# Attention ahead of a mixture of experts on one core: a planner's prices, the port of VectorE and GpSimd in its books, and a margin for attention's matmuls

## The chip, the cores and the metric

The kernel runs on one core of a Trainium2 chip. The metric is the device time of one execution in microseconds; the time before is 980.52 us, the median of 3 runs (980.38 to 980.91).

The engines are named as in the profile: PE is TensorE's matmul queue and PEld its weight loads, DVE is VectorE, ACT is ScalarE, POOL is GpSimd, SP is SyncE, which issues the loads. Each engine takes its instructions in the order of the program and waits for the others by semaphores.

## The reference

Windowed attention with ALiBi biases, and on its output a mixture of four experts whose weights come from given probabilities. All in float32:

```python
B, H, S, D = 4, 8, 576, 64            # q, k, v: (B, H, S, D)
scores = np.matmul(q, k.T) / 8 + slope[h] * -abs(i - j)
scores = np.where((i >= j) & (i - j < 128), scores, -1e9)
attn = softmax(scores)                # rows divided by (sum + 1e-9)
x = np.matmul(attn, v)                # to (2304 tokens, 512)
p = domain_probs / (domain_probs.sum(-1, keepdims=True) + 1e-9)
for e in range(4):                    # w1: (4, 512, 1024), w2: (4, 1024, 512)
    h = np.maximum(x @ w1[e], 0.0)
    out += p[:, e:e + 1] * (h @ w2[e])
```

## The kernel before, in words

**Precision.** A product of two float32 matrices is made of three products in a faster format: every operand is split into a high part (a cast, L278 on ScalarE or L280 on VectorE) and a low part (the difference to the operand, L288, on VectorE or GpSimd), and high by high, high by low and low by high are summed in PSUM. So each weight, each query, key, value, probability and activation costs a cast and a difference on its way to TensorE.

**Tokens and experts.** The 2304 tokens are cut into seven blocks, three of 256 and four of 384. A pass over the weights serves some of the blocks; weights are loaded in 16 units of 256 hidden features (tiles `w1r`, `w2r`, two places each), split (`w1h`, `w1l`, `w2h`, `w2l`) and used. For a unit and a block, `hidden` makes two tiles of hidden features: 12 matmuls in two halves of 6 (L761; the first half needs the heads' pairs 0 and 1, the second half pairs 2 and 3), then ScalarE's relu (L782) and VectorE's low part (L789). `output` multiplies them by w2, 6 matmuls per tile of 128 tokens (L823), and VectorE adds the result, weighted, to an accumulator in SBUF (L840). The first 12 units begin before all of attention is there: units 0 to 6 on block 0 alone, 7 to 11 on blocks 0 and 1, 12 to 15 on blocks 0 to 2. Blocks 3 and 4 share one pass, 5 and 6 the last.

**Attention.** It is done by block and pair of heads, in tiles of 128 queries (72 in all); block 0 works on float32 as it is, the others on split operands. The chain of a tile in `unit` is:

- scores on TensorE (L446; in block 0 L437) into a PSUM bank;
- the scores of the previous tile's keys copied to `s` (L278 or L280), those of its own keys by a predicated copy (L482);
- for each of the two heads, bias and minimum on VectorE (L492), the exponentials and their sums on ScalarE (L504);
- sums plus 1e-9 and their reciprocal on VectorE (L520, L529), then the scaling, in one instruction on VectorE (L536) or in two on ScalarE (L544);
- two transposes on TensorE (L569), high and low part (L278 or L280, L288), and two masked copies on GpSimd into `pt` (L599, L586);
- products with the values on TensorE (L635), summed over the tiles of the segment in PSUM, brought together by ScalarE and VectorE (L658, L661), and split into `xh` and `xl`, which the experts read.

There are three places for `s`, two for the parts, three for `pt`, six PSUM banks for everything but the value products.

**What sets the order.** Nothing is written out by hand. Every operation is first noted with the engines that can do it, an estimate of its time on each, and a due time (`Plan.op`). `Plan.order` then simulates the engines: for each, it looks for the operations that could start first (within `SLACK`, 0.1 us), takes the most urgent by due time, gives an operation that several engines can do to the one that ends it sooner, and records a start. A start is the latest of: the engine being free, the operands being ready (end of each producer plus `GAP`, a passing time by pair of engines, plus `EXTRA`), and a place in the pools being free. Sorted by these starts, the instructions are emitted. The due times of the experts are a running sum of their matmuls' estimated time; those of attention are spread between the times at which blocks are opened, 10 us early (`MARGIN`). The simulation only sets the order: on the chip each engine waits for what its next instruction needs.

The estimates of before are the lines that the change touches:

```python
pool = lambda n: 0.1 + n * 0.0022  # noqa: E731
mm = lambda n: max(n / 2400 + 0.0025, 0.107)  # noqa: E731
```

Of the kernel before, what the change touches and what calls it, by code (L numbers as in the profile page):

```python
# [26 lines left out]
# The operations are noted first, with what they read and write, an estimate of their time and when they are due; a  # L27
# greedy simulation of the engines then sets the order in which they are emitted.
class Buf:
    """A tile of the program: it takes one of its tag's places from its first use to its last."""  # L30
# [8 lines left out]
class Op:  # L39
    __slots__ = ("n", "engs", "emit", "due", "deps", "outs", "wait", "ready", "bufs", "cold", "start", "end", "eng")  # L40


class Plan:
    # What passes from the end of one engine's operation to the start of another's that waits for it.
# [11 lines left out]
    def op(self, engs, emit, due, reads=(), writes=(), holds=(), cold=None):  # L56
        """engs: the engines that can do it, with the time there (us; of a load its bytes)."""
        o = Op()
        o.n, o.engs, o.emit, o.due = len(self.ops), dict(engs), emit, due
        o.deps, o.outs, o.bufs, o.start = set(), [], [], None  # L60
        o.cold = 2 * o.engs.get(PE, 0.0) if cold is None else cold
# [23 lines left out]
    def order(self):  # L85
        at = dict.fromkeys((PE, DVE, ACT, POOL, SP), 0.0)
        queue = {e: [] for e in at}
        bus = 0.0
        owner = {tag: [None] * len(p) for tag, p in self.places.items()}

        def push(o):
            o.ready = {e: max((d.end + EXTRA + self.GAP[d.eng][e] for d in o.deps), default=0.0) for e in o.engs}
            for e in o.engs:
                queue[e].append(o)

        def slots(o):
            """When there are places for what starts with it, and which."""
# [22 lines left out]
        while len(out) < len(self.ops):  # L120
            best = None
            for e, q in queue.items():
                cands, least = [], None
                for o in q:
                    s = slots(o)
                    if s is None:
                        continue
                    t = max(at[e], o.ready[e], s[0] + 0.2 if s[1] else 0.0)
                    cands.append((t, o, s[1]))
                    least = t if least is None else min(least, t)  # L130
# [5 lines left out]
                # Where another engine would end it sooner, it is left to that one.  # L136
# [20 lines left out]
            else:  # L157
                o.end = t + (o.cold if e == PE and t < 10.0 else o.engs[e])
                at[e] = o.end
            new = [b for b in o.bufs if b.place is None]  # L160
# [16 lines left out]
EXTRA = 0.03  # L177

# Time of an instruction on n elements a partition (us).
act = lambda n: 0.05 + n * 0.00087  # noqa: E731  # L180
dve = lambda n: 0.065 + n / 960  # noqa: E731
dve2 = lambda n: 0.065 + n / 1920  # noqa: E731
pool = lambda n: 0.1 + n * 0.0022  # noqa: E731
mm = lambda n: max(n / 2400 + 0.0025, 0.107)  # noqa: E731
mmc = lambda n: max(n / 1200, 0.107)  # noqa: E731

# Blocks of tokens (a pass of the weights takes some of them), and the columns of their group's tile.
# [11 lines left out]
def attention_moe(  # L199
# [14 lines left out]
    P = 128  # L214
# [58 lines left out]
    def cast(o, i, n, due, reads, writes, sbuf=True):  # L273
        """A copy: on ScalarE or VectorE."""
# [7 lines left out]
        plan.op({ACT: act(n), DVE: dve2(n) if sbuf else dve(n)}, emit, due, reads, writes)  # L282

    def minus(o, a, b, n, due, reads, writes, gp=True):
        """A difference: on VectorE, or on GpSimd where both are in SBUF."""
# [4 lines left out]
        plan.op({DVE: dve(n), POOL: pool(n)} if gp else {DVE: dve(n)}, emit, due, reads, writes)  # L290

# [1 line left out]
    # Units of two tiles of hidden features on some blocks of tokens: the first block starts before the others.  # L293
# [21 lines left out]
    def before(t):  # L315
        """How many keys of the tile before a tile's own its scores need; sequences may start in a tile's middle."""
        return min(t * P % S, P)

    # Blocks between whose starts the attention of the next ones is spread.
# [29 lines left out]
    def segment(g):  # L349
        """Loads of the operands, and their high and low parts: queries and keys stacked along the contraction."""  # L350
# [6 lines left out]
        if g.plain:  # L357
            # Both at once: these are what all the others wait for.
# [52 lines left out]
        v4 = lambda: v[:].rearrange("p t (h d) -> p t h d", h=2)[:, :vn]  # noqa: E731  # L411
# [12 lines left out]
    def unit(u):  # L424
# [5 lines left out]
        sv = lambda: s[:, : 2 * P].rearrange("p (h n) -> p h n", h=2) if s.tag == "acc" else s.place  # noqa: E731  # L430
        both = [(s, 0), (s, 1)]
        sc = lambda: bk[:].rearrange("p (h n) -> p h n", h=2)  # noqa: E731
# [21 lines left out]
        # One column for each key of the window: that of the query's tile up to the query, else that of the tile before.  # L454
        # Where a sequence ends in a tile, the queries past it see none of its keys.
# [6 lines left out]
        if pk and (pk < P or edge):  # L462
            plan.op({DVE: 0.28, POOL: 0.3}, clear, d, ["scores"], both)
        qk = [g.q, g.k] if g.plain else [g.qs, g.kh, g.kl]
        passes_ = 8 if g.plain else 4
        plan.op({PE: passes_ * mm(n)}, scores, d, qk, [bk, "scores"], [s], passes_ * mmc(n))
# [23 lines left out]
        # Negated scores and their minimum, the exponentials and their sums.  # L490
# [22 lines left out]
        for h in range(2):  # L513
            keys = [("bias", g.hp)] if pk else [("bias0", g.hp), bk]
            plan.op({DVE: 0.205}, least(h), d + 0.3, keys, [(s, h), (t, h)])
        for h in range(2):
            plan.op({ACT: 0.38}, exponents(h), d + 0.4, [(t, h)], [(s, h), (t, 2 + h)])
        plan.op(
            {DVE: 0.07},
# [499 lines left out]
```

## Time and profile before

| | |
|---|---|
| median of 3 runs | 980.52 us |
| span of the profiled execution | 977.4 us |
| TensorE, matmuls busy | 925.4 us, 95% of the span |
| VectorE busy | 754.0 us, 77% |
| ScalarE busy | 352.2 us, 36% |
| GpSimd busy | 285.6 us, 29% |
| mean granted TensorE clock | 0.995 |

The span runs from the first to the last instruction of the execution that was profiled; the time of a run also holds what lies around it, 3.1 us beside the median. Matmuls overlap in the pipeline, and their ends are modelled, so a row's length is longer than the distance to the next start. A wait is written behind the instruction that waited, with the engine, tile and line that ended it. In a group's row stand the count, the busy time, the mean in ns and the idle time ahead of it.

### The profile page before, as it was taken

To read this page: it belongs to the slowest core of one execution; us is meant where nothing else is said; L and a number is where in the kernel's file an instruction comes from. 1 tells how busy PE (TensorE), PEld (TensorE's weight loads), DVE (VectorE), ACT (ScalarE), POOL (GpSimd) and SP (SyncE) were. 2 spreads that over 40 slices of the span, in tenths; PEclk is the share of its full clock that TensorE was granted. 3 is DMA by queue.
4 is the path that set the end of the run, shared out by engine and by line. 5 is a ranking of instruction groups with operands and counts; after the bars stand their busy time and mean duration, and the time that the engine had idled before them with its cause. 6 is when DMAs were issued, how large, how long until landed. Compare 5 with 4: busy or idle time off the path is not lost.

```text
span 977.4 us, 14432 instructions
## 1 busy us (share of the span) xinstructions
PE 925.4 (95%) x5222; PEld 829.9 (85%) x5222; DVE 754.0 (77%) x1575; ACT 352.2 (36%) x909; POOL 285.6 (29%) x278
## 2 busy tenths in 40 slices
PE   6788898999999999999999999999999999999998
PEld 4677787888888888988888889899999999999997
DVE  5999998898889899888797787866656565656554
ACT  4655445344454555333233432343221212121210
POOL 4667543334434255322232232222101010101000
PEclk9899999999999999999999999999999999999999
DMA  9655433232333345422222211111321121211101
GB/s 235 195 173 171 143 135 114 92 105 84 106 128 117 123 144 191 138 92 83 74 92 82 74 65 58 52 44 65 103 91 66 51 76 46 67 63 65 44 1 65
DMA packets 38359, 95.67 MB, mean 98 GB/s; under 512 B 3728, under 2 KB 15888, under 8 KB 38288
## 3 DMA queue, kind: packets, MB, share of 16 engines
q1 hardware_dynamic: 38288, 94.75, 29.3%
q8 instruction: 41, 0.67, 0.3%
q14 instruction: 30, 0.25, 0.1%
HBM read 90.02 MB, written 4.72 MB: 97 GB/s over the span
## 4 chain that ended last, share of the span: by engine, by line
PE 67%; DVE 26%; issue 3%; DMA 2%; ACT 1%; POOL 1%; DVEq 0%; ACTq 0%; POOLq 0%; SPq 0%
PE b L761 31%; PE b L823 30%; DVE s L492 5%; DVE acc L840 3%; DVE w2l L288 3%; PE av L635 2%; DVE w1l L288 2%; PE b L569 2%; DVE rl L789 2%; DVE qs L288 2%; PE b L446 2%; DVE s L536 1%; DVE s L482 1%; DMA k<-in_qk 1%; DVE x L661 1%
## 5 line engine op out<-in xcount | busy, mean ns | idle before, releaser
L761 PE MATMUL b<-xh,w1h 128*128 128x384 f32 (+1 forms) x896 | 286.8, 320 | 0.0
L761 PE MATMUL b<-xl,w1h 128*128 128x384 f32 (+1 forms) x896 | 281.7, 314 | 0.2 <-DVE xl L288 0.2
L761 PE MATMUL b<-xh,w1l 128*128 128x384 f32 (+1 forms) x896 | 281.7, 314 | 0.0
L840 DVE SCALAR_TENSOR_TENSOR acc<-b,prob,acc 128x512 f32<-128x512 f32 (+1 forms) x271 | 201.7, 745 | 64.9 <-PE b L823 64.2
L782 ACT ACTIVATE rh<-b 128x384 fp32r<-128x384 f32 (+1 forms) x224 | 98.9, 442 | 402.8 <-PE b L761 400.4
L823 PE MATMUL b<-w2l,rh 128*128 128x512 f32 x578 | 227.4, 394 | 0.0
L823 PE MATMUL b<-w2h,rl 128*128 128x512 f32 x578 | 226.9, 393 | 0.0
L823 PE MATMUL b<-w2h,rh 128*128 128x512 f32 x578 | 226.4, 392 | 0.0
L789 DVE SCALAR_TENSOR_TENSOR rl<-b,rh 128x384 fp32r<-128x384 f32 (+1 forms) x224 | 111.0, 495 | 103.8 <-ACT rh L782 102.7
L761 PEld LDWEIGHTS b<-xl,w1h 128*128 128x128 f32 x896 | 170.6, 190 | 5.8 <-DVE xl L288 0.4
L761 PEld LDWEIGHTS b<-xh,w1h 128*128 128x128 f32 x896 | 170.8, 191 | 5.3
L288 POOL TENSOR_TENSOR w1l<-w1r,w1h 128x512 fp32r<-128x512 f32 x60 | 83.6, 1394 | 305.2 <-DVE w1h L280 212.1
L761 PEld LDWEIGHTS b<-xh,w1l 128*128 128x128 f32 x896 | 170.3, 190 | 0.0
L823 PEld LDWEIGHTS b<-w2h,rl 128*128 128x128 f32 x578 | 108.5, 188 | 23.6
L823 PEld LDWEIGHTS b<-w2h,rh 128*128 128x128 f32 x578 | 109.1, 189 | 15.8
L823 PEld LDWEIGHTS b<-w2l,rh 128*128 128x128 f32 x578 | 108.9, 188 | 15.5
L599 POOL TENSOR_SCALAR_AFFINE_SELECT pt<-hl 128x512 fp32r<-128x512 f32 x60 | 42.6, 710 | 235.3 <-DVE hl L288 208.5
L504 ACT ACTIVATE s<-s,t 128x128 f32<-128x128 f32 x128 | 50.8, 398 | 81.8 <-DVE t L492 80.7
L492 DVE CUSTOM_DVE_ANT_0 s<-s,bias 128x128 f32<-128x128 f32 x120 | 75.7, 654 | 1.1
L288 DVE TENSOR_TENSOR w2l<-w2r,w2h 128x512 fp32r<-128x512 f32 x102 | 76.0, 770 | 0.0
L278 ACT ACTIVATE w2h<-w2r 128x512 fp32r<-128x512 f32 x117 | 71.6, 625 | 8.2 <-PE b L823 6.5
L280 DVE CAST w1h<-w1r 128x512 fp32r<-128x512 f32 x92 | 58.8, 653 | 17.5 <-PE b L761 16.2
(89 smaller groups left out, 924.9 us busy)
## 6 DMA issues: line engine op xcount, KB each, us to landing
w1r<-in_w SPq DMA_DIRECT2D x60, 512.0 KB, 3.5
w2r<-in_w SPq DMA_DIRECT2D x60, 512.0 KB, 3.5
q<-in_q SPq DMA_DIRECT2D x16, 384.0 KB, 3.3
k<-in_k SPq DMA_DIRECT2D x12, 512.0 KB, 4.1
k<-in_k SPq DMA_DIRECT2D x12, 384.0 KB, 3.4
out<-acc SPq DMA_DIRECT2D x17, 256.0 KB, 2.0
v<-in_v SPq DMA_DIRECT2D x12, 256.0 KB, 2.7
v<-in_v SPq DMA_DIRECT2D x12, 192.0 KB, 3.0
```

Source lines behind the costliest of these rows:

```text
L278: nc.scalar.activation(o(), i(), AF.Copy)
L280: nc.vector.tensor_copy(o(), i())
L288: by[e].tensor_tensor(out=o(), in0=a(), in1=f(b()), op=ALU.subtract)
L446: nc.tensor.matmul(sc()[:, h, :n], g.qs[:, h, u.q0 : u.q0 + P], m[:, h, u.k0 : u.k0 + n], start=m is g.kh, stop=m is g.kl,)
L492: return lambda e: nc.vector.tensor_tensor_reduce(out=sv()[:, h, :], in0=sv()[:, h, :] if pk else sc()[:, h, :n], in1=(bias if pk else bia ...
L504: return lambda e: nc.scalar.activation(sv()[:, h, :], sv()[:, h, :], AF.Exp, bias=t[:, h : h + 1], scale=-1.0, accum_out=t[:, 2 + h : 3 + h],
L599: nc.gpsimd.affine_select(out=view(dst)[:, :np_, :, o : o + P], in_=f(hl[:, :np_, :, :]), pattern=[[0, 2 * np_], [-1, P]], base=0, channel ...
L761: nc.tensor.matmul(bk[:, :n], a[0][:, kt, fs], b[:, kt, cols], start=kt == 0 and i == 0, stop=kt == KT - 1 and i == 2,)
L782: lambda e: nc.scalar.activation(h[:, :n], bk[:, :n], AF.Relu),
L789: lambda e: nc.vector.scalar_tensor_tensor(out=lo[:, :n], in0=bk[:, :n], scalar=0.0, in1=f(h[:, :n]), op0=ALU.max, op1=ALU.subtract,),
L823: nc.tensor.matmul(bk[:, cs], a[:, ns], b[1][:, fi, cs], start=fi == 0 and j == 0, stop=fi == 1 and j == 2,)
L840: nc.vector.scalar_tensor_tensor(out=o, in0=i_, scalar=p, in1=o, op0=ALU.mult, op1=ALU.add)
```

## The change

Five things are changed in the planner's books; the operations themselves and their operands stay as they are.

- **The port.** An operation has a set `port` of engines on which it holds a port that VectorE and GpSimd share. In the simulation it can then only start when the port is free, and holds it to its end. By default it is held by what runs on GpSimd; casts from SBUF hold it on VectorE, differences of two SBUF operands on both, the minimum (where it reads SBUF) and the scaling on VectorE; the clearing of `s` and differences with PSUM hold nothing.
- **The margin.** `late` is added to the time at which an operation's operands count as ready. It is `LATE`, 1.5 us, for the scores, the transposes and the value products of all blocks but block 0.
- **TensorE's price.** `mm` goes from 0.1625 to 0.1736 us for 384 columns, from 0.2158 to 0.2314 for 512. The due times, which are sums of it, stretch with it.
- **GpSimd's price** for a difference goes from 1.23 to 1.41 us at 512 elements.
- **Small prices:** the minimum 0.205 to 0.216, the sums and the reciprocal 0.07 and 0.08 to 0.19, the scaling on ScalarE 0.59 to 0.62.

Comments are left out as well, which moves line numbers by 8 to 13.

```diff
-    def op(self, engs, emit, due, reads=(), writes=(), holds=(), cold=None):
+    def op(self, engs, emit, due, reads=(), writes=(), holds=(), cold=None, port=None, late=0.0):
...
+        o.port, o.late = (POOL,) if port is None else port, late
...
-            o.ready = {e: max((d.end + EXTRA + self.GAP[d.eng][e] for d in o.deps), default=0.0) for e in o.engs}
+            o.ready = {e: max((d.end + EXTRA + self.GAP[d.eng][e] for d in o.deps), default=0.0) + o.late for e in o.engs}
...
                     t = max(at[e], o.ready[e], s[0] + 0.2 if s[1] else 0.0)
+                    if e in o.port:
+                        t = max(t, port)
...
                 at[e] = o.end
+                if e in o.port:
+                    port = o.end
...
+LATE = 1.5
...
-pool = lambda n: 0.1 + n * 0.0022  # noqa: E731
-mm = lambda n: max(n / 2400 + 0.0025, 0.107)  # noqa: E731
+pool = lambda n: 0.1 + n * 0.00256
+mm = lambda n: max(n * 0.000452, 0.112)
...
-        plan.op({ACT: act(n), DVE: dve2(n) if sbuf else dve(n)}, emit, due, reads, writes)
+        plan.op(
+            {ACT: act(n), DVE: dve2(n) if sbuf else dve(n)}, emit, due, reads, writes, port=(DVE,) if sbuf else ()
+        )
...
-        plan.op({DVE: dve(n), POOL: pool(n)} if gp else {DVE: dve(n)}, emit, due, reads, writes)
+        engs = {DVE: dve(n), POOL: pool(n)} if gp else {DVE: dve(n)}
+        plan.op(engs, emit, due, reads, writes, port=(DVE, POOL) if gp else ())
...
-            plan.op({DVE: 0.28, POOL: 0.3}, clear, d, ["scores"], both)
+            plan.op({DVE: 0.28, POOL: 0.3}, clear, d, ["scores"], both, port=())
...
-        plan.op({PE: passes_ * mm(n)}, scores, d, qk, [bk, "scores"], [s], passes_ * mmc(n))
+        late = 0.0 if g.plain else LATE
+        plan.op({PE: passes_ * mm(n)}, scores, d, qk, [bk, "scores"], [s], passes_ * mmc(n), late=late)
...
-            plan.op({DVE: 0.205}, least(h), d + 0.3, keys, [(s, h), (t, h)])
+            plan.op({DVE: 0.216}, least(h), d + 0.3, keys, [(s, h), (t, h)], port=(DVE,) if pk else ())
...
-            {DVE: 0.07},
+            {DVE: 0.19},
...
-            {DVE: 0.08},
+            {DVE: 0.19},
...
-        plan.op({DVE: dve(2 * P), ACT: 0.59}, weights_, d + 0.7, [(t, 4)], both)
+        plan.op({DVE: dve(2 * P), ACT: 0.62}, weights_, d + 0.7, [(t, 4)], both, port=(DVE,))
...
-        plan.op({PE: 2 * mm(P)}, transposed, d + 0.8, [*both, "ident"], [bk2, "transposed"], [hl], 2 * mmc(P))
+        plan.op({PE: 2 * mm(P)}, transposed, d + 0.8, [*both, "ident"], [bk2, "transposed"], [hl], 2 * mmc(P), late=late)
```

How this moves instructions is seen at three places. In the names, the number behind a tile's name is its place in the pool, `b` are PSUM banks, `av` the sums of the value products.

**TensorE, the end of block 1's attention.** Before, the last value products of block 1 stand ahead of six output products, and those ahead of the next transposes:

```order
L635 MATMUL av_131<-pt_87,vs_74 128x256 x2
L635 MATMUL av_132<-pt_87,vs_74 128x256 x2
L635 MATMUL av_131<-pt_88,vs_74 128x128 x2
L635 MATMUL av_132<-pt_88,vs_74 128x128 x2
L823 MATMUL b_130<-w2h_103,rh_107 128x512
L823 MATMUL b_130<-w2l_105,rh_107 128x512
L823 MATMUL b_130<-w2h_103,rl_111 128x512
L823 MATMUL b_130<-w2h_103,rh_108 128x512
L823 MATMUL b_130<-w2l_105,rh_108 128x512
L823 MATMUL b_130<-w2h_103,rl_112 128x512
L569 MATMUL b_126<-ident,s_77 128x128 x2
```

Now the same value products (L647) stand between the two halves of block 1's first hidden tile, in bank 130, with the transposes of two tiles of block 2 right behind them. The scores of `s_75`, a tile with 192 keys, stand six products ahead of the first value products:

```order
L774 MATMUL b_130<-xl_93,w1h_100 128x256
L774 MATMUL b_130<-xh_91,w1l_102 128x256
L647 MATMUL av_131<-pt_87,vs_74 128x256 x2
L647 MATMUL av_132<-pt_87,vs_74 128x256 x2
L647 MATMUL av_131<-pt_88,vs_74 128x128 x2
L647 MATMUL av_132<-pt_88,vs_74 128x128 x2
L581 MATMUL b_126<-ident,s_77 128x128 x2
L581 MATMUL b_127<-ident,s_75 128x128 x2
L774 MATMUL b_130<-xh_91,w1h_100 128x256
L774 MATMUL b_130<-xl_93,w1h_100 128x256
L774 MATMUL b_130<-xh_91,w1l_102 128x256
```

The experts' first work on block 1 has moved up against the end of block 1's attention.

**TensorE, the first long run of expert products.** Before, the transposes of the first split tile, `s_75`, stand ahead of the products that finish block 0's first hidden tile (bank 128):

```order
L446 MATMUL b_126<-kl_72,qs_68 128x256
L569 MATMUL b_127<-ident,s_75 128x128 x2
L446 MATMUL b_129<-kh_70,qs_68 128x256
L446 MATMUL b_129<-kl_72,qs_68 128x256
L446 MATMUL b_129<-kh_70,qs_68 128x256
L446 MATMUL b_129<-kl_72,qs_68 128x256
L761 MATMUL b_128<-xh_91,w1h_99 128x256
L761 MATMUL b_128<-xl_93,w1h_99 128x256
L761 MATMUL b_128<-xh_91,w1l_101 128x256
```

Now the products follow the scores (the hidden tile is in bank 125):

```order
L457 MATMUL b_127<-kh_70,qs_68 128x256
L457 MATMUL b_127<-kl_72,qs_68 128x256
L457 MATMUL b_127<-kh_70,qs_68 128x256
L457 MATMUL b_127<-kl_72,qs_68 128x256
L774 MATMUL b_125<-xh_91,w1h_99 128x256
L774 MATMUL b_125<-xl_93,w1h_99 128x256
L774 MATMUL b_125<-xh_91,w1l_101 128x256
```

The transposes of `s_75` have moved behind 24 expert products.

**VectorE, an edge tile of block 2.** Before, between the minimum and the next weight difference, VectorE casts `xh`, and scales the tile itself (L536):

```order
L280 CAST xh_91<-x_89 128x256
L789 SCALAR_TENSOR_TENSOR rl_111<-b_129,rh_107 128x256
L288 TENSOR_TENSOR xl_93<-x_89,xh_91 128x256
L840 SCALAR_TENSOR_TENSOR acc_121<-b_127,prob,acc_121 128x512
L520 TENSOR_SCALAR t_79<-t_79 128x2
L529 RECIPROCAL t_79<-t_79 128x2
L536 TENSOR_TENSOR s_75<-s_75,t_79 128x256
L280 CAST w1h_100<-w1r_96 128x512
L789 SCALAR_TENSOR_TENSOR rl_112<-b_130,rh_108 128x256
L288 TENSOR_TENSOR w1l_102<-w1r_96,w1h_100 128x512
```

Now the same tile's sums and reciprocal (L532, L541) are not followed by a scaling:

```order
L532 TENSOR_SCALAR t_79<-t_79 128x2
L288 CAST vs_74<-v_66 128x3x2x64
L541 RECIPROCAL t_79<-t_79 128x2
L674 TENSOR_TENSOR x_89<-av_131,x_89 64x256
L674 TENSOR_TENSOR x_89<-av_132,x_89 64x256
L288 CAST w1h_100<-w1r_96 128x512
L298 TENSOR_TENSOR xl_93<-x_89,xh_91 128x256
L802 SCALAR_TENSOR_TENSOR rl_112<-b_130,rh_108 128x256
L853 SCALAR_TENSOR_TENSOR acc_117<-b_127,prob,acc_117 128x512
L298 TENSOR_TENSOR w1l_102<-w1r_96,w1h_100 128x512
```

The scaling and the cast of `xh` have gone to ScalarE, the cast of values has come from there.

More of the change, by code (lines that the diff above doesn't have):

```diff
@@ L39 @@
 class Op:
-    __slots__ = ("n", "engs", "emit", "due", "deps", "outs", "wait", "ready", "bufs", "cold", "start", "end", "eng")
+    __slots__ = ("n", "engs", "emit", "due", "deps", "outs", "wait", "ready", "bufs", "cold", "start", "end", "eng", "port", "late")
 class Plan:
@@ L87, in order @@
         queue = {e: [] for e in at}
-        bus = 0.0
+        bus = port = 0.0
         owner = {tag: [None] * len(p) for tag, p in self.places.items()}
         def push(o):
-            o.ready = {e: max((d.end + EXTRA + self.GAP[d.eng][e] for d in o.deps), default=0.0) for e in o.engs}
+            o.ready = {e: max((d.end + EXTRA + self.GAP[d.eng][e] for d in o.deps), default=0.0) + o.late for e in o.engs}
             for e in o.engs:
@@ L653, in unit @@
                 sum((8 if g.plain else 4) * mmc(j[3]) for j in jobs),
+                late=late,
             )
```

## The prediction

> **What bounds the kernel now.** I read the profile's page first, then TensorE's waits, then the chain of waits and the timeline around one of them. The page says that TensorE (PE) is the engine that is nearly always busy, and that VectorE (DVE) is nearly as full for the first half:
>
> ```profile
> span 977.4 us, 14432 instructions
> ...
> PE 925.4 (95%) x5222; PEld 829.9 (85%) x5222; DVE 754.0 (77%) x1575; ACT 352.2 (36%) x909; POOL 285.6 (29%) x278
> ...
> PE   6788898999999999999999999999999999999998
> ...
> DVE  5999998898889899888797787866656565656554
> ```
>
> From 645 us on nothing but expert products runs, back to back. That stretch gives the price of PE's work: twelve products of 512 columns (L823) take 2.76 us, 0.230 us each, and twelve of 384 (L761) 2.10 us, 0.175 each. The change does not alter the number or the shape of any matmul, so it cannot touch this time. It can only touch PE's waits.
>
> ```profile
> 771.95 2.76 PE b L823 x12
> 774.72 2.10 PE b L761 x12
> ```
>
> TensorE's waits, each row with total, times and longest; the first two rows are from 0 to 50 us, the next three from 50 us to the end, the last is the part of the third that lies behind 420 us:
>
> ```profile
> PE b L437 <- DMA k<-in_qk: 6.8, 2, 4.5
> PE b L569 <- DVE s L536: 1.9, 1, 1.9
> PE b L569 <- DVE s L536: 29.6, 27, 2.9
> PE av L635 <- POOL pt L599: 3.3, 6, 1.5
> PE b L569 <- ACT s L544: 2.2, 3, 1.4
> PE b L569 <- DVE s L536: 9.2, 11, 1.4
> ```
>
> Behind 50 us PE waits 29.6 + 3.3 + 2.2 = 35.1 us in 36 pieces, and every one is attention work standing in PE's queue before its operand is there: transposes (L569) of probabilities that VectorE or ScalarE has not scaled yet, and products with the values (L635) that GpSimd has not masked yet. Engines take their queues in order, so expert products that are ready stand behind them. 9.2 us fall behind 420 us, 25.9 before.
>
> Each such wait costs more than its figure. In the timeline below, products of 512 columns start 0.23 apart, but the wait is counted from the end of the last one, 0.39 after its start: 0.16 us of the pipeline's tail is not in the wait.
>
> ```profile
> 169.43 0.39 PE L823 MATMUL b<-w2l,rh 128*128 128x512 f32 x1
> 169.66 0.39 PE L823 MATMUL b<-w2h,rl 128*128 128x512 f32 x1
> 172.84 0.66 PE L569 MATMUL b<-ident,s 128*128 128x128 f32 x2 [2.79 <-DVE s L536]
> ```
>
> Behind this wait of 2.79 us the chain of waits shows a further price: twelve products of 256 columns take 2.56 us, and the next twelve 1.48.
>
> ```profile
> 173.50 2.56 PE b L761 x12
> ...
> 178.81 1.48 PE b L761 x12
> ```
>
> That is 1.1 us lost to a slower TensorE clock; at 149.98 us, behind a wait of about the same length, it did not happen. [...]
>
> Why was the operand late there? VectorE's minimum (L492) and GpSimd's difference ran in the same moments:
>
> ```profile
> 166.02 2.71 POOL L288 TENSOR_TENSOR kl<-k,kh 128x1024 fp32r<-128x1024 f32 x1
> 166.41 2.48 DVE L492 CUSTOM_DVE_ANT_0 s<-s,bias 128x128 f32<-128x128 f32 x1
> 170.75 1.26 POOL L288 TENSOR_TENSOR w1l<-w1r,w1h 128x512 fp32r<-128x512 f32 x1 [2.02 <-ACT w1h L278]
> 171.12 0.91 DVE L520 TENSOR_SCALAR t<-t 128x2 f32<-128x2 f32 x1
> L492 DVE CUSTOM_DVE_ANT_0 s<-s,bias x120: 272/292/2491, 35.4 to 686.7; 128x128 f32<-128x128 f32 x120
> ```
>
> L492 starts inside GpSimd's operation and ends 0.16 us after it. The last row gives least, median and longest of that line: 0.272, 0.292 and 2.491 us. So half of them run in 0.29 and a few are held for two. The old planner knows nothing of this and puts the transpose where it believes the probabilities to be ready.
>
> **The change part by part.** *The margin and the new prices.* The planner holds attention's PE operations back until 1.5 us after the moment it believes them ready, and fills in expert products. How much cover this really makes I counted along PE's order, with the prices above: the PE work between a tile's scores and its transposes was 6.0 us in the mean over blocks 1 to 4 and 5.6 over blocks 5 and 6; it becomes 8.2 and 7.7. (Scores and transposes are paired in their order.) In a typical late place, 6 products of 384 that stood behind the transposes now stand ahead of them: 6 x 0.175 = 1.05 us more. From transposes to value products the median cover goes from 3.2 to 4.9. The growth of about 2.1 us stands against a mean wait of 35.1 / 36 = 0.98 and a longest of 2.9. Were the chain on the other engines unchanged, two waits of 2.9 would leave 0.8 each and nothing else would be left. I do not take it so: PE going faster asks more of VectorE per microsecond, and late tiles gain only 1.05. I leave a fifth of the waits, 7 us in about 10 pieces (bounds: nothing, and 70% of the part ahead of 420 us, see the second rival). **Gain 28.1 us, 26 x 0.16 = 4.2 of tails, and the 1.1 of the slow clock.**
>
> *VectorE's load.* With the port in its books, the planner gives work away. By the order, of w1h's casts VectorE keeps 68 of 92, of w2l's differences 88 of 102, of w1l's 55 of 60, of the scalings of a tile 23 of 49. The prices:
>
> ```profile
> L288 DVE TENSOR_TENSOR w2l<-w2r,w2h 128x512 fp32r<-128x512 f32 x102 | 76.0, 770 | 0.0
> L280 DVE CAST w1h<-w1r 128x512 fp32r<-128x512 f32 x92 | 58.8, 653 | 17.5 <-PE b L761 16.2
> L536 DVE TENSOR_TENSOR s<-s,t 128x256 f32<-128x256 f32 x42 | 21.7, 516 | 1.2
> L544 ACT ACTIVATE s<-s,t 128x128 f32<-128x128 f32 x44 | 15.3, 394 | 8.4 <-DVE t L529 7.5
> ```
>
> 24 x 0.653 + 14 x 0.770 + 26 x 0.516, and five of w1l at w2l's price, make 15.7 + 10.8 + 13.4 + 3.9 = 44 us; smaller groups go both ways and give some 8 back. No gain of its own is booked for it: VectorE is not the end of the chain, but it pays for the cover's holding. ScalarE, at 36%, takes the casts beside PE's work. Where it scales, a tile's chain takes 2 x 0.394 = 0.79 for 0.52, 0.27 longer, inside the cover's growth. GpSimd's differences go from 126 to 135. Loads change places on SP's queue by one to three; behind 50 us PE waits for no load, so I take that at nothing, and were a load late it would show as a cast waiting.
>
> *The start.* Here the first tile's transposes no longer stand ahead of the first long run of expert products:
>
> ```profile
> 39.37 0.58 PE L569 MATMUL b<-ident,s 128*128 128x128 f32 x2 [1.93 <-DVE s L536]
> ```
>
> **Gain 1.9 us.** Ahead of that the DMA waits of 6.8 stay, since the loads of q and k for block 0 keep their places.
>
> *The entry of block 1 (new cost).* In the new order the transposes of block 2's first tile with 192 keys stand 1.9 us of PE work behind its scores (6 products, 8 value products, one pair of transposes), and the second half of block 1's first hidden tile only two pairs of transposes behind the last value products it depends on. Before, there were 6.1 us in the second place. The nearest rows for the two chains:
>
> ```profile
> 104.58 0.28 PE L446 MATMUL b<-kl,qs 128*128 128x192 f32 x1
> 111.06 0.41 PE L569 MATMUL b<-ident,s 128*128 128x128 f32 x2 [0.55 <-DVE s L536]
> 95.60 1.36 PE L635 MATMUL av<-pt,vs 128*128 128x256 f32 x8
> 101.91 0.73 POOL L288 TENSOR_TENSOR xl<-x,xh 128x256 fp32r<-128x256 f32 x1 [0.23 <-DVE xh L280]
> ```
>
> Scores to transposes took 111.06 - 104.86 = 6.2 us, so PE stands 6.2 - 1.9 = 4.3. Value products to the finished low parts took 102.64 - 96.96 = 5.7; 4.3 + 0.5 of it has passed by then, so 0.9 more. After over 5 us of standing I add the 1.1 of the slow clock. **Cost 6.3 us** (bounds: 0 if VectorE is far ahead; 11 if the chain takes 10). At block 2's entry the cover falls from 10.3 to 4.3 against the same 5.7: between 0 and 1.4, I take **0.7**.
>
> **The sum**, against the profiled execution: 977.4 - 28.1 - 4.2 - 1.1 - 1.9 + 6.3 + 0.7 = 949.1 us of span. The runs' median, 980.52, is 3.1 above the profiled span, what lies around it; kept, that gives **952 us**.
>
> **The rivals.** *All waits go (8 in 100).* The cover's growth beats all but two waits, and a lighter VectorE may reach block 1 early: 977.4 - 35.1 - 5.8 - 1.1 - 1.9 + 3.1 = 937 us.
>
> *VectorE is the bound of the first 400 us (13 in 100).* For it speaks the stretch of 60 to 100 us:
>
> ```profile
> 60.00:100.00 40.00, 34.92 (x230) 30.36 (x229) 39.56 (x90) 22.73 (x65) 27.41 (x23) 1.00 0.49 160
> ```
>
> VectorE (third pair of columns) is busy 39.56 of 40 us. If it cannot go faster, cover only moves where PE waits. Then 70% of the 25.9 us stays (gain 7.8), 7.2 of the late 9.2 goes, 15 tails with it (2.4): 977.4 - 7.8 - 7.2 - 2.4 - 1.9 + 7.0 + 3.1 = 968 us. Against it: 36 us of its work are gone, and its busy time contains the holds by GpSimd.
>
> *Slower: the holds grow (9 in 100).* GpSimd gets more differences of weights, and VectorE's minimum, scaling and small L520 stand behind them. One hold like that at 166.41 adds 2.48 - 0.29 = 2.2 us to a tile's chain. The planner keeps the two apart only as far as its times hold, and it books no port for L520, which the trace shows held for 0.91. If the mean chain grows by 2.0 us, about one more hold a tile, the cover's growth is spent and the entry's cost decides: from there the time is above 980. At 2.6 the 36 waits get 0.5 longer: 977.4 + 18 - 1.9 + 7.5 + 3.1 = 1004 us. Against it: fewer of VectorE's operations with two operands in SBUF are left to be held. [...]
>
> *The change does not do what it says (4 in 100).* Planner's times are not chip times; the waits could move to the value products and the block entries, and the sum stay: 980 us. Against it stand the covers counted above.
>
> **How the numbers follow.** The forecast's own case has the remaining 66 in 100, about 938 to 962 us by its bounds (no waits left with the entry paid: 977.4 - 35.1 - 5.8 - 1.1 - 1.9 + 7.0 + 3.1 = 944, and some 6 less if the entry is hidden; 11 at the entry and a third of the waits left: 977.4 - 23.4 - 3.8 - 1.1 - 1.9 + 11.7 + 3.1 = 962). With the rivals at 937 and 968 the range is 934 to 971 us; the cases at 980 and 1004 are left out. Measurements of this kernel tell about 0.2% apart, 2 us: faster 0.87, the same 0.04, slower 0.09.
>
> **What would show it.** In the profile after: TensorE's waits at the transposes and value products behind 50 us fall from 35.1 to about 7; one wait of 3 to 7 us stands at the transposes or at the hidden products' low parts near 95 us, with twelve slow products behind it; L492's mean falls towards its median 0.29; VectorE's busy time falls by 30 us or more; PE's last stretch is unchanged. I am wrong if the waits at the transposes keep 15 us or more (VectorE's bound), if L492 or the scalings get longer (holds), or if PE waits more than 10 us for low parts (the entries).

## The result, and the profile after

Median of 4 runs: 956.6 us (955.57 to 957.36), against 980.71 for the kernel before, measured beside it: a ratio of 0.9754, 95% interval 0.9739 to 0.9770. The profiled execution took 955.57 us, its span is 953.9. I had forecast 952 us, 934 to 971.

The head of the page of the changed kernel, with three of its rows of tenths:

```profile
span 953.9 us, 14358 instructions
PE 921.0 (97%) x5222; PEld 833.9 (87%) x5222; DVE 719.2 (75%) x1528; ACT 376.6 (39%) x977; POOL 283.3 (30%) x283
...
PE   6798799999999999999999999999999999999998
...
DVE  4899998888889989878787787776665656656553
...
PEclk9799899999999999999999999999999999999999
```

From the sixth slice on (119 us) TensorE's row has nothing but nines up to the last slice. What is left of holes lies in the first five, and there VectorE stands at nine from the third on.

TensorE's waits behind 50 us in the changed kernel (total, times, longest):

```profile
PE b L581 <- DVE s L548: 6.8, 3, 4.7
PE b L581 <- ACT s L556: 4.7, 4, 2.0
PE b L457 <- DVE kl L298: 1.9, 1, 1.9
PE b L774 <- DVE w1l L298: 1.4, 2, 0.8
PE b L774 <- POOL w1l L298: 0.6, 1, 0.6
PE av L647 <- DVE x L674: 0.4, 1, 0.4
```

35.1 us in 36 pieces have become 15.8 in 12. 11.5 of them stand at the transposes, none at the masked copies. Behind 110 us, which turns out to be the place where the two kernels part, the rows of before come first, then those of after:

```profile
PE b L569 <- DVE s L536: 24.3, 23, 2.9
PE b L569 <- ACT s L544: 1.9, 2, 1.4
PE av L635 <- POOL pt L599: 1.2, 3, 0.6
```

```profile
PE b L581 <- ACT s L556: 2.3, 2, 2.0
PE b L581 <- DVE s L548: 1.8, 1, 1.8
PE b L774 <- DVE w1l L298: 0.6, 1, 0.6
```

27.4 us in 28 pieces against 4.7 in 4: 22.7 us, and 24 tails of 0.16 make 3.8, together 26.5. The span fell by 23.5, so by 110 us the changed kernel must be some 3 us behind. Each kernel's row for its first 110 us says so too (before, then after; the pairs are PE, PEld, DVE, ACT, POOL, busy us and instructions):

```profile
0.00:110.00 110.00, 88.79 (x501) 74.56 (x502) 98.62 (x255) 61.03 (x176) 67.98 (x71) 0.97 0.61 188
```

```profile
0.00:110.00 110.00, 85.36 (x472) 72.12 (x473) 90.36 (x233) 70.18 (x198) 64.18 (x72) 0.92 0.59 182
```

TensorE has done 472 matmuls where it had done 501, and 3.4 us less of busy time; at 0.16 each, the 29 would be 4.6 us, so the lag is between 3 and 5. Most of it stands at **the entry of block 1**. The timeline of the changed kernel there:

```profile
103.28 1.27 POOL L298 TENSOR_TENSOR w2l<-w2r,w2h 128x512 fp32r<-128x512 f32 x1
103.36 1.33 DVE L504 CUSTOM_DVE_ANT_0 s<-s,bias 128x128 f32<-128x128 f32 x1
104.51 1.85 POOL L298 TENSOR_TENSOR kl<-k,kh 128x768 fp32r<-128x768 f32 x1
104.63 2.01 DVE L548 TENSOR_TENSOR s<-s,t 128x256 f32<-128x256 f32 x1
106.79 0.66 PE L581 MATMUL b<-ident,s 128*128 128x128 f32 x2 [4.65 <-DVE s L548]
109.19 0.77 PE L581 MATMUL b<-ident,s 128*128 128x128 f32 x2 [1.75 <-ACT s L556]
```

TensorE stands 4.65 and 1.75 us, 6.4 in all. The second pair of transposes is that of the tile with 192 keys, the first that of the tile ahead of it. Twice in a row a step of VectorE (the minimum of the 192-key tile, then the scaling of the tile ahead) starts inside a GpSimd difference and ends 0.14 and 0.28 us after it. Behind the stop TensorE's granted clock is 0.50 (109.0 to 111.2 us) and 0.56 (to 113.6 us), then 1.00 again. The chain of waits shows what this costs, and a little later the usual pace:

```profile
109.96 1.28 PE b L774 x6
111.24 2.39 PE b L836 x6
...
118.27 1.43 PE b L774 x12
119.70 1.39 PE b L836 x6
```

Six products of 256 columns take 1.28 us instead of 0.72, six of 512 columns 2.39 instead of 1.39: 1.6 us lost.

The groups of VectorE that were to be freed of holds: the minimum and the sums' addition before, then these and the scaling after (that of before, 516 ns, stands in the prediction):

```profile
L492 DVE CUSTOM_DVE_ANT_0 s<-s,bias 128x128 f32<-128x128 f32 x120 | 75.7, 654 | 1.1
L520 DVE TENSOR_SCALAR t<-t 128x2 f32<-128x2 f32 x72 | 16.3, 227 | 9.9 <-ACT s L504 9.0 <-ACT acc L504 0.7
```

```profile
L504 DVE CUSTOM_DVE_ANT_0 s<-s,bias 128x128 f32<-128x128 f32 x120 | 60.0, 528 | 0.7
L532 DVE TENSOR_SCALAR t<-t 128x2 f32<-128x2 f32 x72 | 24.8, 344 | 12.4 <-ACT s L516 11.4 <-ACT acc L516 0.7
L548 DVE TENSOR_TENSOR s<-s,t 128x256 f32<-128x256 f32 x20 | 14.5, 723 | 0.5
```

The minimum's mean fell from 654 ns to 528, nowhere near the 292 that was its median. The sums' addition rose from 227 to 344, the scaling from 516 to 723 (with 20 left of 42).

### The profile page after: what moved, and what is told of

The parts are those of the page before. It is cut to its first block, busy times and chain, and to the rows that moved or that the text cites. A ratio compares the mean times of both kernels' runs of the same rounds, so it can differ in the third digit from the quotient of the medians.

```text
span 953.9 us, 14358 instructions
## 1 busy us (share of the span) xinstructions
PE 921.0 (97%) x5222; PEld 833.9 (87%) x5222; DVE 719.2 (75%) x1528; ACT 376.6 (39%) x977; POOL 283.3 (30%) x283
## 4 chain that ended last, share of the span: by engine, by line
PE 87%; DVE 9%; ACT 2%; DMA 1%; issue 1%; ACTq 0%
PE b L836 39%; PE b L774 39%; PE av L647 4%; PE b L457 3%; DVE s L504 2%; PE b L581 2%; DVE acc L853 1%; DMA k<-in_qk 1%; DVE w2l L298 1%; PE b L448 1%; DVE t L532 1%; DVE s L548 1%; DVE rl L802 1%; DVE vs L298 1%; DVE x L674 0%
## 5 line engine op out<-in xcount | busy, mean ns | idle before, releaser
L836 PE MATMUL b<-w2h,rh 128*128 128x512 f32 x578 | 229.1, 396 | 0.0
L298 POOL TENSOR_TENSOR w1l<-w1r,w1h 128x512 fp32r<-128x512 f32 x65 | 87.3, 1345 | 294.2 <-DVE w1h L288 207.4
L298 DVE TENSOR_TENSOR w2l<-w2r,w2h 128x512 fp32r<-128x512 f32 x88 | 65.0, 770 | 2.5 <-ACT w2h L286 2.4
L298 POOL TENSOR_TENSOR w2l<-w2r,w2h 128x512 fp32r<-128x512 f32 x32 | 43.4, 1360 | 66.4 <-ACT w2h L286 53.8
L504 DVE CUSTOM_DVE_ANT_0 s<-s,bias 128x128 f32<-128x128 f32 x120 | 60.0, 528 | 0.7
```

What stands on the lines that cost most here:

```text
L298: by[e].tensor_tensor(out=o(), in0=a(), in1=f(b()), op=ALU.subtract)
L504: return lambda e: nc.vector.tensor_tensor_reduce(out=sv()[:, h, :], in0=sv()[:, h, :] if pk else sc()[:, h, :n], in1=(bias if pk else bia ...
L836: nc.tensor.matmul(bk[:, cs], a[:, ns], b[1][:, fi, cs], start=fi == 0 and j == 0, stop=fi == 1 and j == 2,)
```

## The experiments

My theory: the cover does it, PE work placed between a tile's scores and its transposes. The expectations call this theory 1. The rivals: the port in the books does it, by shorter holds and less work on VectorE (theory 2); prices nearer to the measured times do it (theory 3). Later two questions came up: why two changes of price cost so much, and how large the holds are. In the order of a kernel, "cover" is the mean PE work between scores and transposes over blocks 1 to 4 and 5 to 6, in us, counted as in the prediction (before 5.9/5.6, after 8.1/7.7 by the count used for this table). Medians and intervals are of the runs; the next three columns come from the profiles, the cover from the orders.

| kernel | median, us | ratio (95%) | matmuls by 110 us | PE's waits behind 110 us (pieces) | minimum, mean ns | cover |
|---|---|---|---|---|---|---|
| before | 980.71 | 1 | 501 | 27.4 (28) | 654 | 5.9/5.6 |
| after | 956.6 | 0.9754 (0.9739–0.9770) | 472 | 4.7 (4) | 528 | 8.1/7.7 |
| margin alone | 957.41 | 0.9768 (0.9747–0.9789) | 475 | 8.0 (8) | 589 | 7.6/6.7 |
| prices alone | 998.93 | 1.0180 (1.0165–1.0195) | 463 | 34.1 (32) | 612 | 5.7/5.7 |
| port alone | 963.36 | 0.9830 (0.9802–0.9858) | 516 | 15.7 (19) | 636 | 7.1/6.1 |
| port and prices | 980.02 | 0.9987 (0.9971–1.0002) | 496 | 21.1 (24) | 655 | 6.9/5.8 |
| margin and prices | 963.84 | 0.9832 (0.9810–0.9855) | 470 | 10.5 (11) | 496 | 7.1/7.3 |
| margin and port | 945.13 | 0.9650 (0.9626–0.9675) | 494 | 0.8 (2) | 564 | 9.1/7.8 |
| after, block 1 later | 951.74 | 0.9710 (0.9694–0.9727) | 484 | 4.2 (5) | 564 | 8.8/7.8 |
| after, port for the sums | 948.91 | 0.9682 (0.9665–0.9698) | 485 | 2.3 (2) | 542 | 9.2/8.0 |
| before, TensorE's price alone | 993.58 | 1.0131 (1.0107–1.0155) | 471 | 32.7 (27) | 610 | 5.6/5.1 |
| after, no GpSimd differences | 943.01 | 0.9613 (0.9587–0.9638) | 508 | 0.0 (0) | 321 | 7.6/7.6 |
| after, margin 3 us | 947.55 | 0.9663 (0.9635–0.9690) | 491 | 0.0 (0) | 529 | 9.8/9.1 |
| after, TensorE's old price | 942.19 | 0.9606 (0.9581–0.9630) | 509 | 0.4 (1) | 551 | 9.7/8.4 |

**The parts alone.** First the margin without port and prices, in the kernel before, for the same scores, transposes and value products:

```diff
+LATE = 1.5
-            o.ready = {e: max((d.end + EXTRA + self.GAP[d.eng][e] for d in o.deps), default=0.0) for e in o.engs}
+            o.ready = {e: max((d.end + EXTRA + self.GAP[d.eng][e] for d in o.deps), default=0.0) + o.late for e in o.engs}
```

> The kernel before with the margin of 1.5 us alone; old prices, no port. Theory 1 (the margin's cover takes the waits away): most of the 24 us gained, 955 to 964 us, TensorE's waits at the transposes behind 50 us under 15 us, though VectorE's operations are held as often as before (mean of the minimum near 0.65 us). Theory 2 (the port in the books does it, by fewer holds and less work on VectorE): 972 to 982 us. Theory 3 (the right price of a matmul does it): 972 to 982 us.

It measured 957.41 us: alone, the margin gives what the whole change gives. The first of its waits behind 50 us:

```profile
PE b L572 <- DVE s L539: 8.9, 6, 3.1
PE b L572 <- ACT s L547: 2.5, 2, 1.7
```

VectorE is busy 757.1 us here, more than before, and its minimum still means 589 ns. Nor did a tile's way become shorter: by the traces, the time from the end of its scores to the end of its scaling is 6.3 us before, 6.7 with the margin alone and 7.1 in the changed kernel (means of the 64 tiles of blocks 1 to 6). The waits go because work stands in between, not because VectorE has less to do. The margin acts on scores, transposes and value products at once; no run takes these three apart.

All the new prices without port and margin, in the kernel before (the diff shows three of them):

```diff
-pool = lambda n: 0.1 + n * 0.0022
-mm = lambda n: max(n / 2400 + 0.0025, 0.107)
+pool = lambda n: 0.1 + n * 0.00256
+mm = lambda n: max(n * 0.000452, 0.112)
...
-            {DVE: 0.07},
+            {DVE: 0.19},
```

> The kernel before with the new prices alone; no margin, no port. Theory 1: 974 to 986 us, the waits at the transposes stay near 30 us. Theory 2: the same. Theory 3: 956 to 966 us.

998.93 us, 18 slower, and none of the three theories had it (974 to 986 us, or 956 to 966): prices nearer to the measured durations make a worse program. The minimum is shorter than before (612 for 654), and yet the waits behind 50 us grow:

```profile
PE b L569 <- DVE s L536: 34.6, 20, 4.3
PE b L569 <- ACT s L544: 7.4, 11, 1.5
```

The mean cover, 5.7/5.7, is hardly below that of before, and the way from scores to scaling is 0.3 us longer (6.6). A lost cover explains this run only in part.

The port without margin and prices, as an edit of the changed kernel; the small prices go back too:

```diff
-LATE = 1.5
+LATE = 0.0
...
-pool = lambda n: 0.1 + n * 0.00256
-mm = lambda n: max(n * 0.000452, 0.112)
+pool = lambda n: 0.1 + n * 0.0022
+mm = lambda n: max(n / 2400 + 0.0025, 0.107)
```

> The kernel after with a margin of 0 and the old prices, so the port alone. Theory 1: 970 to 984 us; a few us may be gained since VectorE gives some 40 us of work away. Theory 2: 956 to 966 us and the mean of the minimum under 0.45 us. Theory 3: 970 to 984 us.

963.36 us. Theory 1 missed this: the time is 6.6 us below its range and inside that of theory 2. But theory 2's sign, a minimum under 450 ns, did not come. The port alone does help, and not by what it is named for: the minimum's mean hardly fell,

```profile
L504 DVE CUSTOM_DVE_ANT_0 s<-s,bias 128x128 f32<-128x128 f32 x120 | 73.3, 636 | 0.8
```

while the cover rose to 7.1/6.1 and VectorE's busy time fell to 717.3 us. The way from scores to scaling did not get shorter (7.2 us for 6.3). My reading is that a planner that counts the port believes VectorE later, so it puts the transposes later and gives work away: a margin by another road. No run takes the cover and the work given away apart.

**One part taken out.** Without the margin:

```diff
-LATE = 1.5
+LATE = 0.0
```

> The kernel after with the margin at 0: port and prices together. Theory 1: 970 to 980 us, waits at the transposes behind 50 us of 20 us or more. Theories 2 and 3: 955 to 962 us, no more than a few us lost against the kernel after; the entry of block 1 may then lose its wait of 6.4 us and be faster still.

980.02 us (10 runs, 975.12 to 982.30; the profile is of the fastest of them): no change against before, at the edge of theory 1's range, with 24.2 us of waits at the transposes behind 50 us. Port (−17) and prices (+18.6) cancel. The mean cover alone does not give the time: port alone (7.1/6.1) and port and prices (6.9/5.8) are close in it and 17 us apart.

Without the port:

```diff
                     t = max(at[e], o.ready[e], s[0] + 0.2 if s[1] else 0.0)
-                    if e in o.port:
-                        t = max(t, port)
```

> The kernel after without the port: margin and prices. After four runs theory 1 reads: the time follows the PE work that stands between a tile's scores and its transposes, and the margin, the port and the old low price of a matmul each make such cover. Counted along the order it is here 7.1 us in the mean over blocks 1 to 4 and 7.3 over 5 and 6 (after: 8.1 and 7.7; margin alone: 7.6 and 6.7). Theory 1: 955 to 966 us. Theory 2 (the port's books matter by what they take off VectorE): VectorE busy 750 us again, 966 to 978 us.

963.84 us, 7 slower than after, although its minimum is shorter (496 against 528). The time is in theory 1's range, and VectorE's load is what theory 2 said. With the port the cover is larger and VectorE has 32 us less to do (719.2 against 751.3); this run does not tell which of the two counts.

Without the new prices, the small ones included:

```diff
-pool = lambda n: 0.1 + n * 0.00256
-mm = lambda n: max(n * 0.000452, 0.112)
+pool = lambda n: 0.1 + n * 0.0022
+mm = lambda n: max(n / 2400 + 0.0025, 0.107)
```

> The kernel after with the old prices: margin and port. The cover is 9.1 and 7.8 us, and the two transposes at the entry of block 2 have 7.1 and 10.4 us where the kernel after has 7.1 and 1.8. Theory 1: 943 to 952 us, faster than the kernel after; TensorE's waits behind 50 us under 8 us. Theory 3 (right prices make a right plan): slower than the kernel after, 960 us or more.

945.13 us, 11 faster than after: beside margin and port, the prices cost what they were thought to refine.

**Which price, and the entry.** TensorE's price alone, in the kernel before:

```diff
-mm = lambda n: max(n / 2400 + 0.0025, 0.107)
+mm = lambda n: max(n * 0.000452, 0.112)
```

> The kernel before with the new price of a matmul alone. The cover falls from 5.9 and 5.6 to 5.6 and 5.1 us: the old price was 7% too low, so the plan put 7% more matmuls into a chain's time than fit, and that was a margin nobody had named. If so, 988 to 1003 us, near the 999 of all the prices together. If the loss of the prices came from the others (GpSimd's difference, the small operations), 977 to 984 us.

993.58 us, 13 of the 18 that all prices cost. Its waits at the transposes behind 50 us:

```profile
PE b L569 <- DVE s L536: 23.2, 15, 3.7
PE b L569 <- ACT s L544: 15.4, 11, 2.8
```

The old price was 6 to 7% below the 0.230 and 0.175 us that the products take. A planner that believes TensorE faster than it is puts more products in front of a tile's transposes; on the chip these take 7% longer and give the tile that much more time. With the right price the cover falls from 5.9/5.6 to 5.6/5.1, while the way from scores to scaling does not get longer (6.1 us for 6.3). So the error acted as a margin that nobody had named. That this is all of it is not shown: the due times are sums of the same price and stretch with it, and no run changes the one without the other.

The reverse, only TensorE's price taken back in the changed kernel:

```diff
-mm = lambda n: max(n * 0.000452, 0.112)
+mm = lambda n: max(n / 2400 + 0.0025, 0.107)
```

> The kernel after with the old price of a matmul only; margin, port and the other new prices stay. Cover 9.7 and 8.4 us, 8.3 and 6.9 at the entry of block 2. Theory 1: 940 to 948 us, level with the run with all old prices (945) or a little faster. If the price of GpSimd's difference and the small ones matter by the load that they move, it differs from that run by over 5 us.

942.19 us, with the margin and port: the best of all, not told apart from 943.01 below. Its waits behind 50 us sum to 5.8 us, the longest 1.9, and its first 110 us hold 37 matmuls more than after's.

A larger margin at the right price:

```diff
-LATE = 1.5
+LATE = 3.0
```

> The kernel after with a margin of 3.0 us. Cover 9.8 and 9.1 us in the mean, but 4.6 and 1.1 at the entry of block 2. Theory 1 with nothing else: 943 to 950 us. With the qualification that a longer chain starves PE at the block entries, as the kernel after shows: the waits at the transposes behind 130 us near 0, those between 90 and 130 us over 8 us, 951 to 962 us.

947.55 us, as forecast without the qualification. Behind 130 us nothing waits at all. The entry still does, but with 5.4 us from 90 to 130 us it stays under the 8 that I had feared, most of it here:

```profile
PE b L581 <- ACT s L556: 3.6, 2, 2.7
```

Eight units of weights on block 0 alone instead of seven, so that block 1 is needed one unit later:

```diff
-EARLY = (7, 12)
+EARLY = (8, 12)
```

> The kernel after with EARLY (8, 12): eight units instead of seven run on block 0 alone before block 1 is needed. The number of weight loads is the same. If the entry of block 1 is what the kernel after still loses (4.65 and 1.75 us of waits, the slow clock behind them), 946 to 951 us and no wait over 2.5 us between 95 and 125 us. If the stop there only shows that VectorE is behind (the rival that VectorE bounds the first 100 us), the wait moves on and the time stays at 954 to 958 us.

951.74 us, 4.9 faster, just outside the forecast. From 95 to 125 us the stop at the transposes is gone, but the waits there are not less: 6.7 us for 6.4, most of them at two other places:

```profile
PE av L647 <- DVE x L674: 2.7, 1, 2.7
PE b L774 <- DVE w1l L298: 2.5, 1, 2.5
```

Both wait for VectorE, which is busy 5.00 of the 5 us from 100 to 105 us. Around 100 us VectorE is behind, whatever TensorE asks it for; in this the rival was right. The time fell nevertheless, but not at the entry: behind 125 us the waits are 1.2 us where they were 4.7, with a cover of 8.8/7.8.

**The holds.** The port also held by the sums' addition, which had none:

```diff
         plan.op(
             {DVE: 0.19},
+            port=(DVE,),
```

> The kernel after with the port also held by the addition to the two sums (line 532), which the trace shows held by GpSimd for up to 1.7 us and which the plan leaves free. If the books keep VectorE and GpSimd apart on the chip, the mean of that line falls from 0.34 to under 0.22 us. If drift from the plan makes the books useless for that (as the minimum's mean, 0.64 us with the port alone and 0.65 before, says), it stays above 0.25 us, and what changes is the cover: 9.2 and 8.0 us, with 6.4 and 10.4 us at the entry of block 2. Theory 1: 945 to 952 us in either case.

948.91 us, 7.7 faster, but the addition still takes 292 ns in the mean (344 after, 227 before) and the minimum 542 (528). The gain goes with a cover of 9.2/8.0; the books don't keep the two engines apart.

All differences on VectorE; GpSimd keeps the masked copies and the clearing:

```diff
-        engs = {DVE: dve(n), POOL: pool(n)} if gp else {DVE: dve(n)}
+        engs = {DVE: dve(n)}
```

> The kernel after with every difference on VectorE and none on GpSimd, which keeps its masked copies and memsets. If GpSimd's differences hold VectorE's operations with two operands in SBUF, the mean of the minimum falls from 0.53 to 0.28 to 0.33 us, that of the sums from 0.34 to 0.15 to 0.18, and the scaling runs at 0.42. If GpSimd's masked copies hold them as well, the minimum stays above 0.40. VectorE then has some 100 us more to do: 960 to 1000 us, bound by it for the first 400.

943.01 us. I had expected VectorE to be overrun, and was wrong. From its page and its groups:

```profile
PE 916.0 (98%) x5222; PEld 830.5 (88%) x5222; DVE 726.8 (77%) x1656; ACT 372.8 (40%) x961; POOL 90.9 (10%) x154
```

```profile
L504 DVE CUSTOM_DVE_ANT_0 s<-s,bias 128x128 f32<-128x128 f32 x120 | 34.7, 321 | 0.7
L532 DVE TENSOR_SCALAR t<-t 128x2 f32<-128x2 f32 x72 | 12.9, 179 | 7.7 <-ACT s L516 6.8 <-ACT acc L516 0.7
L298 DVE TENSOR_TENSOR w1l<-w1r,w1h 128x512 fp32r<-128x512 f32 x120 | 81.5, 681 | 0.0
L298 DVE TENSOR_TENSOR w2l<-w2r,w2h 128x512 fp32r<-128x512 f32 x120 | 80.8, 697 | 0.3 <-ACT w2h L286 0.2
```

GpSimd executes 129 instructions fewer (154 for 283): its 135 differences are gone, and six more clearings have come to it. VectorE executes 128 more (1656 for 1528). 97 of the differences are weights' low parts (65 of w1l, 32 of w2l), at 0.68 and 0.70 us 67 us of work; the other 38 add some 33 us at this version's means. Yet VectorE's busy time rises by 7.6 us, 719.2 to 726.8. What paid for it are the holds: 25.3 us less in the minimum, 11.9 less in the addition, 15 in the casts of w1h (70, at 425 ns for 645), and the rest in the other casts and differences. So nearly all of the holds come from GpSimd's differences, since the masked copies and clearings are still there and the minimum's mean, 321, is near its median of 284. The port stands in the plan's books; what the runs show is which groups are held. Two large ones that read PSUM are not: the differences of `hl` mean 418 ns before and after and 417 here, those of `rl` with 384 columns 554, 554 and 555. The way from scores to scaling is 6.0 us where it was 7.1: in this version it is the way that became shorter, not the cover that grew.

**Two quantities that go with the time.** In the chain of waits shown above, 18 matmuls of the early stage take 1.43 + 1.39 = 2.82 us (the rows at 118.27 and 119.70), 0.16 each. Adding to each span 0.16 for every matmul done by 110 us, and taking off the waits behind 110 us and 0.16 per piece, leaves 1020 to 1032 us for all 14 kernels, whose spans run from 938.9 to 997.1. So most of the spread is in these two: how far TensorE got by 110 us, and what it waits afterwards. This says where the time is, not why. What remains grows with the waits (1020 to 1022 where there are none, 1030 to 1032 where there are over 30 us); I put it down to clock and short waits without having shown it. (The matmuls by 110 us are of several widths, so 0.16 is a mean; each of the 14 profiles has the same 5222 matmuls.)

## Why the prediction was right, and where its sizes were off

The median came out 4.6 us above the forecast, the profiled span 4.8 above the forecast span of 949.1. Split at 110 us: of the sum, 1.9 (start) + 0.8 x 7.7 (waits from 50 us on) + 1.1 (their tails) − 6.3 (entry) put the kernel 2.9 us ahead there; it was 3.0 behind (23.5 − 26.5). So the sum erred by 5.9 us ahead of that place, and by 1.1 the other way behind it. Of the 3.1 us that the sum adds for what lies around the span, 1.7 to 2.1 do, by the later runs that have both figures (1.7 in the changed kernel's profile); the rest is that the profiled execution of before was shorter than the median one.

- **The margin's cover: right, and shown.** Behind 110 us I had left a fifth of 27.4, 5.5 us; 4.7 are there. The tails came out at 24 pieces instead of 26. Behind 420 us 9.2 us of waits became 0.3. The margin alone gives the whole gain, with VectorE as loaded as before. The fifth was a guess and not worked out, so that it came this close is in part luck. The reason given for it, that the way from scores to scaling would not stay unchanged, holds: it grew by 0.8 us (6.3 to 7.1) against 2.2 of cover.
- **The entry of block 1: right in place, in mechanism for the larger part, and dearer.** I had 4.3 + 0.9 of waits and 1.1 of slow clock near 95 us; it was 4.65 + 1.75 and about 1.6, near 107. The 192-key tile with its small cover is there, but its way took 8.6 us (from 100.53 to 109.15) and not 6.2. The 4.65 stand ahead of it, at a tile with some 7 us of cover whose way took 11.6 (from 94.99 to 106.64), which I had not foreseen. The 0.9 for the hidden products' low parts did not come: they start behind the transposes without a wait.
- **The start: wrong.** The 1.9 us were to be gained. The waits of the first 50 us stayed at 13.2 (13.3 before). The transposes did move, but what stands there now waits in their place:

```profile
PE b L448 <- DMA k<-in_qk: 6.8, 2, 4.5
PE b L774 <- DVE xh L288: 2.9, 1, 2.9
PE b L581 <- ACT acc L556: 1.7, 1, 1.7
```

The step that failed is "the first tile's transposes no longer stand ahead of the first long run": true, but the hidden products need `xh`, which comes off the same busy engines. I had asked what goes, and not what is late next.

- **From 60 to 110 us the second rival was right.** I gave "VectorE is the bound" to the first 400 us, 13 in 100. In the changed kernel VectorE is busy 37.19 of the 40 us from 60 to 100 us, and the row from 100 to 110 us has it at 9.73 of 10 us and TensorE at 3.60. For the first 50 us, where VectorE is busy 33.65 us, it is not shown.

```profile
100.00:110.00 10.00, 3.60 (x25) 2.98 (x24) 9.73 (x23) 6.19 (x18) 6.50 (x7) 0.82 0.50 170
```

From 50 us to the entry 4.7 us are left (1.9 of them for `kl`, 1.8 for the low parts of weights and for `x`, which I had not foreseen), where a fifth of 7.7 was in the sum. With the start's 1.8 and the entry's 1.2 of waits and 0.5 of clock, this makes about 6.7, near the 5.9. Afterwards the bound gives way: TensorE's row of tenths has no hole, and VectorE falls to eight and later seven tenths.

- **VectorE's load: right.** 44 less 8 were 36 us; it fell by 34.8, 754.0 to 719.2.
- **The holds: wrong in size, without effect on the sum.** I expected the minimum's mean to fall towards 292; it fell to 528. Per group, count times what the mean is above the undisturbed 0.285, 0.15 and 0.42 us (median, least and median in the version without GpSimd's differences), the holds in minimum, addition and scaling were 44 + 5.5 + 4 = 54 us before and 29 + 14 + 6 = 49 after. One sign of being wrong did come, the scalings got longer (516 to 723 ns), and so did the addition (227 to 344). But there were 20 scalings for 42, the sum of the holds fell, and the third rival ("holds grow", with a time above 980) did not come true, though the timeline at 103 us has its mechanism: the plan meant to keep the engines apart, the chip ran them together. In the pairs of rows at 103.28 and 104.51 the GpSimd difference was there first, by 0.08 and 0.12 us, and the VectorE step ended 0.14 and 0.28 us after it.
- **"Does not do what it says": in part.** The new prices, which look like a correction, cost 11 us in the changed kernel (956.6 against 945.13) and 18 in that of before. I had put prices and margin into one term and so could not see that they work against each other.
- **Two readings.** The prediction has nothing but expert products from 645 us on; in the kernel before 48 of attention's matmuls start behind that point, the last at 694 us. The prices were read at 772 us, so they stand. And the 1.1 us of slow clock were put behind the entry's stop as if they had to come; that was an estimate from one place. In the kernel before, the stop of 2.79 us that ended at 172.84 us was followed by a granted clock of 0.51 (173.50 to 176.06 us), the longer one of 2.86 us that ended at 149.98 us by 1.00 (149.5 to 152.8 us). Behind the entry's stop the clock did fall, to 0.50. What decides it, no run shows.

Still open: why the entry takes its particular form under each setting (the covers there were not forecast one by one), whether the price of a matmul acts by the cover alone or also by the due times, and what the version without GpSimd's differences gives together with TensorE's old price or a larger margin; that was not tried.

## What to carry to other kernels

When a static order is planned from durations, put the safety in openly: a margin ahead of what the busiest engine would stand at (here TensorE, whose waits behind 50 us went from 35.1 to 15.8), with other ready work in between. A price that is too low for that engine can be such a margin in disguise; here correcting it without adding one made the program 13 us slower. And after a stall is taken away, ask at each place what is late next; not asking was 6 us of error here.

## What the runs showed that I had not expected

- Moving all 135 differences, 97 of them of 128x512, from GpSimd to a VectorE that was busy 75% of the time raised its busy time by 7.6 us and made the program 13.6 us faster (956.6 to 943.01). GpSimd's help cost VectorE nearly as much as it saved.
- The hold also hits the smallest operations: the addition on 128x2 elements ran 1.25 us at 94.24 us in the changed kernel, beside a GpSimd difference that began at 93.39 and ended 0.03 us ahead of it, against a mean of 179 ns without such differences. (The first row merges two differences.)

```profile
93.39 3.32 POOL L298 TENSOR_TENSOR w1l<-w1r,w1h 128x512 fp32r<-128x512 f32 x2
94.24 1.25 DVE L532 TENSOR_SCALAR t<-t 128x2 f32<-128x2 f32 x1
```
